# Linear attention feeding an MLP on one core: small per-head matmuls put into 64x64 quarters of the TensorE array

## The chip, the core and the metric

The kernel runs on one core of a Trainium2 chip. The metric is device time in microseconds for one execution. Before the change it is 293.32 us (median of three runs, 293.12 to 293.63). Line numbers such as L199 are lines of the kernel before the change, as the profile names them. PE is TensorE (PEld its weight loads), DVE is VectorE, ACT is ScalarE, POOL is GpSimd, SP is SyncE.

## What is computed

There are 8 batches of 8 heads, each with 576 tokens of 64 dimensions. Linear attention is followed by two dense layers with a tanh-shrink between them.

```python
phi = lambda x: np.where(x > 0, x, np.exp(x) - 1.0) + 1.0
q_p, k_p = phi(q), phi(k)
kv  = einsum('bhsd,bhse->bhde', k_p, v)          # 64x64 per head
z   = k_p.sum(axis=2)                            # 64 per head
num = einsum('bhsd,bhde->bhse', q_p, kv)
den = einsum('bhsd,bhd->bhs', q_p, z) + 1e-06
x   = (num / den) as 4608 tokens x 512 (head, dim)
h   = x @ w_in                                   # 512 -> 2048
out = (h - tanh(h)) @ w_out                      # 2048 -> 512
```

## The kernel before

**The dense part** runs over nine chunks `c` of 512 tokens. Layer 1 (`l1mm`, L366) makes 16 slices `fi` of 128 features, each from four 128x512 matmuls over the head pairs `p`; ACT takes the tanh of two slices at once (L372) and DVE subtracts (L373). Layer 2 (`l2mm`, L387) then makes four token blocks of 128 in 16 steps `s` of four matmuls each; ACT copies a finished block out (L396) and SP sends it (L401). One layer of one chunk is 64 matmuls.

**The attention part** runs over eight batches of 576 tokens and is slipped into the dense stream by hand. The lists `s1[fi]` and `s2[s]` say which pieces are issued after which slice of layer 1 or step of layer 2. Every engine works through its own instructions in program order, so the place in these lists is the place in each engine's queue. Chunk 0 carries batch 1; chunk `c` from 1 to 6 carries batch `c+1`; batch 0 comes before everything.

On the chip a batch lies as two partition halves (`hg`), two groups `i`, and two heads `h` beside each other, so its eight heads are (hg, i, h). The pieces that the change touches are these:

- **kv** (`a_kv_cols`, L199; for batch 1 `a_kv`, L177; for batch 0 `b0_kv`, L221, and `b0_z`, L210). For each group and each of nine token strips, two matmuls stand side by side in the array, one per partition half: 64 rows of contraction, 128 columns of weights (both heads of the strip), and both heads' `v` as the moving side. The result holds four 64x64 blocks of which two mix different heads. DVE multiplies it with a 0/1 `mask` (L202, L186, L225, L214) into `kz`, which takes the mixed blocks out. Each `v` carries columns of ones, so that z comes out as further columns. There are 36 such matmuls per batch.
- **den** (`a_den`, L276): sixteen matmuls of 32 weight columns, four side by side; DVE adds 1e-6 (L281) and takes the reciprocal (L285). `a_spread` sends it through DRAM and back to all partitions (`rdb`, L305 and L308); batch 1 splits it (`a_split`, L295 to L298) and spreads it with matmuls (L354).
- **num** (`num_mm`, L317 and L320; batch 0 L231): for each head pair `p` one 128x128x512 matmul whose weights are the masked `kz`, and four 64-column matmuls for the last 64 tokens. `a_num` issues pair after pair, one per layer-2 step (`s` 9 to 13, in chunk 1 `s` 12 to 15), in PSUM banks 6 and 7 in turn; DVE scales each into `xT` (L328, L333). For batch 1, ACT copies the five results (L344, L346).

**PSUM** has eight banks, `ps_all[:, 0..7]`. Dense work takes banks 0 to 5 in rotation, attention takes 6 and 7. In chunk 0 the side work takes 4 to 7 in rotation.

**Loads** are issued by POOL. `load_wi` (L110) loads `w_in` with two transfers per column slice, one for each 64 partitions, because a pair `p` holds head rows that lie 256 apart.

## Time and profile before

| | |
|---|---|
| median of three runs | 293.32 us |
| profiled execution: first to last instruction (its span) | 291.64 us |
| granted TensorE clock, mean | 0.999 |
| PE busy | 284.7 us (98%) |
| DVE, ACT, POOL busy | 175.1, 139.8, 34.0 us |
| dense matmuls L366 and L387 | 127.5 and 127.3 us busy |
| kv, batches 2 to 7 (L199) | 216 matmuls, 7.4 us busy |
| num (L317) | 28 matmuls, 10.1 us busy |
| num, last 64 tokens (L320) | 32 matmuls, 2.2 us busy |

Only the span of the profiled execution is on the page, and no time of its own around it; the median stands 1.68 us above the span. Busy times of PE count pipelined matmuls, which overlap, so a group's share of the path is read from where its first matmul and the next group's first matmul start, not from its mean duration. A wait is put down to the engine or transfer that ended last before it.

### The profile page before, as it was taken

Reading aid. Unit: us, or ns where it says so; the run is one execution under the profiler, and the core shown is the slowest. Engines: PE = TensorE matmul, PEld = TensorE weight load, DVE = VectorE, ACT = ScalarE, POOL = GpSimd, SP = SyncE. Lnnn points to the kernel's source line nnn. Section 1 sums busy time; section 2 is a strip of 40 time slices with the busy share of each in tenths; the row PEclk is TensorE's granted clock in tenths of the full one; section 3 lists DMA queues with packets and bytes.
Section 4 is the critical chain, followed back from the end, with each engine's and each line's share of the span. In section 5 each row is a group of like instructions: output and inputs, shape, how many; then the busy total and the mean of one; then the engine's idle time right before and its main releaser. Section 6 shows DMA issues by size and latency. Waiting matters only on the chain.

```text
span 291.6 us, 4505 instructions
## 1 busy us (share of the span) xinstructions
PE 284.7 (98%) x1803; PEld 134.4 (46%) x1803; DVE 175.1 (60%) x266; ACT 139.8 (48%) x168; POOL 34.0 (12%) x56
## 2 busy tenths in 40 slices
PE   7899999999999999999999999999999999999994
PEld 2544464454454444444454444444544444444443
DVE  4759968987468674776478637865581457106600
ACT  4838557846354734465345534751551155126411
POOL 8575030110030003000300030000000000000000
PEclk9999999999999999999999999999999999999999
DMA  6999999997998768965895579666117310130032
GB/s 98 192 203 213 207 205 211 212 180 141 257 165 152 176 127 136 197 145 123 136 223 125 122 138 197 136 150 139 31 38 165 73 36 0 42 84 20 0 74 72
DMA packets 39093, 38.94 MB, mean 134 GB/s; under 512 B 16352, under 2 KB 33824, under 8 KB 38304
## 3 DMA queue, kind: packets, MB, share of 16 engines
q0 software_dynamic: 17568, 18.35, 39.0%
q1 hardware_dynamic: 21344, 20.17, 30.7%
q8 instruction: 14, 0.23, 0.3%
q10 hardware_dynamic: 160, 0.13, 0.1%
q14 instruction: 7, 0.06, 0.1%
HBM read 43.91 MB, written 9.55 MB: 183 GB/s over the span
## 4 chain that ended last, share of the span: by engine, by line
PE 82%; DMA 13%; POOL 2%; ACT 1%; issue 1%; SPq 0%; DVE 0%; POOLq 0%
PE ps_all L366 38%; PE ps_all L387 37%; DMA v<-in_v_dram 6%; DMA w_in_sb<-in_moe_w_in_dram 3%; DMA kraw<-in_k_dram 2%; DMA out_dram<-osb 2%; PE ps_all L199 2%; PE ps_all L317 2%; PE ps_all L276 1%; POOL v L419 1%; ACT osb L396 1%; PE ps_all L177 1%; SPq L401 0%; POOL qraw L90 0%; PE ps_all L320 0%
## 5 line engine op out<-in xcount | busy, mean ns | idle before, releaser
L366 PE MATMUL ps_all<-xT,w_in_sb 128*128 128x512 bf16 x574 | 127.5, 379 | 0.0
L387 PE MATMUL ps_all<-w_out_sb,gT 128*128 128x512 bf16 x560 | 127.3, 379 | 0.0
L373 DVE TENSOR_TENSOR gT<-ps_all,th 128x1024 bf16<-128x1024 f32 x64 | 77.9, 1218 | 59.5 <-ACT th L372 59.5
L372 ACT ACTIVATE th<-ps_all 128x1024 f32<-128x1024 f32 x64 | 65.6, 1025 | 57.3 <-PE ps_all L366 47.2
L366 PEld LDWEIGHTS <-w_in_sb 128*128 128x128 bf16 x574 | 55.0, 98 | 66.0
L387 PEld LDWEIGHTS <-gT 128*128 128x128 bf16 x560 | 54.2, 98 | 64.5
L396 ACT COPY osb<-ps_all 128x512 f32<-128x512 f32 (+1 forms) x36 | 20.9, 583 | 71.8 <-PE ps_all L387 52.6
L328 DVE TENSOR_TENSOR xT<-ps_all,rdb 128x512 bf16<-128x512 f32 x24 | 16.5, 691 | 13.7 <-PE ps_all L317 11.2
L134 ACT ACTIVATE e<-qraw 128x1152 bf16<-128x1152 bf16 x16 | 18.5, 1161 | 8.5 <-DMA qraw<-in_q_dram 8.5
L134 ACT ACTIVATE e<-kraw 128x1152 bf16<-128x1152 bf16 x15 | 17.4, 1163 | 0.5 <-DMA kraw<-in_k_dram 0.5
L136 DVE TENSOR_TENSOR qp<-e,r 128x1152 bf16<-128x1152 bf16 x16 | 12.1, 759 | 8.0 <-ACT e L134 7.2
L136 DVE TENSOR_TENSOR kp<-e,r 128x1152 bf16<-128x1152 bf16 x15 | 11.4, 758 | 7.9 <-ACT e L134 7.0
L383 POOL COPY g<-qT 1x1 bf16<-1x1 bf16 x5 | 0.9, 178 | 118.9 <-DMA qT<-qp 118.9
L378 DVE TENSOR_TENSOR gT<-ps_all,th 128x512 bf16<-128x512 f32 x16 | 10.3, 686 | 2.4 <-ACT th L377 1.7
L377 ACT ACTIVATE th<-ps_all 128x512 f32<-128x512 f32 x16 | 9.2, 599 | 4.4 <-PE ps_all L366 3.2
L317 PE MATMUL ps_all<-qT,kz 128*128 128x512 bf16 x28 | 10.1, 379 | 0.0
L447 PE MATMUL ps_all<-zero 128*128 128x512 bf16 x29 | 8.2, 441 | 1.2 <-DVE zero L405 1.2
L135 DVE TENSOR_SCALAR r<-qraw 128x1152 bf16<-128x1152 bf16 x16 | 7.3, 454 | 2.1 <-DMA qraw<-in_q_dram 2.1
L199 PEld LDWEIGHTS <-kp 64*128 64x128 bf16 x216 | 6.4, 94 | 2.5 <-issue 2.5
L285 DVE RECIPROCAL rden<-den 128x144 f32<-128x144 f32 x7 | 7.4, 1053 | 0.2
L199 PE MATMUL ps_all<-vp,kp 64*128 64x136 bf16 x216 | 7.4, 220 | 0.0
L394 DVE COPY osb<-ps_all 128x128 f32<-128x128 f32 x1 | 0.3, 292 | 11.6 <-DMA out_dram<-osb 11.6
(85 smaller groups left out, 123.5 us busy)
## 6 DMA issues: line engine op xcount, KB each, us to landing
out_dram<-osb SPq DMA_DIRECT2D x70, 128.0 KB
rdb<-ds SPq DMA_DIRECT2D x12, 576.0 KB
kraw<-in_k_dram POOLq DMA_DIRECT2D x7, 576.0 KB, 6.7
qraw<-in_q_dram POOLq DMA_DIRECT2D x7, 576.0 KB, 8.8
v<-in_v_dram POOLq DMA_DIRECT2D x7, 576.0 KB, 11.8
w_in_sb<-in_moe_w_in_dram POOLq DMA_DIRECT2D x6, 256.0 KB, 8.8
w_out_sb<-in_moe_w_out_dram POOLq DMA_DIRECT2D x3, 512.0 KB, 14.3
qraw<-in_q_dram POOLq DMA_DIRECT2D x2, 288.0 KB, 4.6
```

Source lines behind the costliest of these rows:

```text
L134: return (lambda: nc.scalar.activation(e, x, AF.Exp), lambda: nc.vector.tensor_scalar(r, x, 0.0, 1.0, ALU.max, ALU.add), lambda: nc.vector ...
L136: lambda: nc.vector.tensor_tensor(y, e, r, ALU.min))
L199: nc.tensor.matmul(ps[hg][:, i, :], kp[r, i, j].rearrange("p h d -> p (h d)"), vp[r, i, j, :], start=(j == 0), stop=(j == J - 1))
L317: nc.tensor.matmul(ps, kz[:, p // 2, p % 2, 0:128], qT[:, p % 2, 0:8, p // 2, :], start=True, stop=True)
L328: nc.vector.tensor_mul(xT[:, p, S * b:S * b + 512].rearrange("p (j t c) -> p j t c", j=8, t=4), ps.rearrange("p j (t c) -> p j t c", t=4), ...
L366: nc.tensor.matmul(h, w_in_sb[:, 2 * (p % 2) + p // 2, fi * 128:(fi + 1) * 128], xT[:, p, c * 512:(c + 1) * 512], start=(n == 0), stop=(n ...
L372: nc.scalar.activation(th, h, AF.Tanh)
L373: nc.vector.tensor_sub(gT[:, fi:fi + 2, :], h, th)
L377: nc.scalar.activation(th, h, AF.Tanh)
L378: nc.vector.tensor_sub(gT[:, fi, :], h, th)
L387: nc.tensor.matmul(o, gT[:, fi, i * 128:(i + 1) * 128], w_out_sb[:, fi, :], start=(fi == 0), stop=(fi == NF - 1))
L396: nc.scalar.copy(osb[:, f0:f1], o[:, f0:f1])
```

## The change

The kv, z and num matmuls now work on one head each. A matmul has 64 rows and 64 columns of the array, and four of them, one per quarter, are issued after each other: two partition halves by two heads for kv and z, two heads by two partition halves for num. What used to be 36 matmuls of kv per batch are 72; what used to be 4 + 4 of num are 8 + 8. No block mixes heads any more, so `kz` is a plain copy and only the 32 columns for den are still multiplied with the (smaller) mask, now as two DVE operations for both halves together. `vp` holds 66 columns per head, the last two of ones.

`a_num` issues all matmuls of a batch in one place: the 8 large ones into banks 0 to 3, the 8 small ones into banks 6 and 7, and then all five DVE operations (after step `s` 9, in chunk 1 after `s` 12). Layer 2 takes banks 4 and 5 in turn, layer 1 takes bank `fi % 6`. In chunk 0 the order of the pieces after step 8 is den, the last tokens of batch 0, then num of batch 1, with the banks given below. A pair `p` now holds heads 2p and 2p+1, so `w_in` is loaded in its own row order with one transfer per slice, and the mask is filled for the new order. One of the two memsets of ones beside `v` (POOL, L419) is dropped, since only batch 1 still reads them.

```diff
     def load_wi(f0, n):
-        for h in range(2):
-            nc.gpsimd.dma_start(out=w_in_sb[64 * h:64 * h + 64, :, f0:f0 + n],
-                                in_=moe_w_in[256 * h:256 * h + 256, f0:f0 + n].rearrange(
-                                    "(t d) f -> d t f", d=64))
+        nc.gpsimd.dma_start(out=w_in_sb[:, :, f0:f0 + n],
+                            in_=moe_w_in[:, f0:f0 + n].rearrange("(t p) f -> p t f", p=128))
...
+    def quads():
+        return [(slice(64 * r, 64 * r + 64), slice(64 * c, 64 * c + 64), r, c) for c in range(2) for r in range(2)]
+
+    def kv_mm(b, v_of, ps_of):
         kp = kp_t[b]
         for i in range(2):
             for j in range(J):
-                for hg in range(2):
-                    r = slice(64 * hg, 64 * hg + 64)
-                    nc.tensor.matmul(ps[hg][:, i, :], kp[r, i, j].rearrange("p h d -> p (h d)"),
-                                     vp[r, i, j, :], start=(j == 0), stop=(j == J - 1))
-        for hg in range(2):
-            nc.vector.tensor_mul(kz_t[b][:, hg, :, 0:136], ps[hg], mask[:, hg, :, 0:136])
+                for rs, cs, hg, h in quads():
+                    nc.tensor.matmul(ps_of(cs, hg, i), kp[rs, i, j, h, :], v_of(rs, h, i, j),
+                                     start=(j == 0), stop=(j == J - 1))
...
+    def a_kv_cols(b, b0):
+        kz_t[b] = kz_c[b % 2]
+        kv_mm(b, lambda rs, h, i, j: vp[rs, i, j, h, :],
+              lambda cs, hg, i: ps_all[cs, b0 + hg, 66 * i:66 * i + 66])
+        ps = ps_all[:, b0:b0 + 2, 0:132].rearrange("p g (i e) -> p g i e", i=2)
+        nc.vector.tensor_mul(kz_t[b][:, :, :, 64:96], ps[:, :, :, 64:65].to_broadcast([128, 2, 2, 32]), mask)
+        nc.vector.tensor_copy(kz_t[b][:, :, :, 0:64], ps[:, :, :, 0:64])
...
+    def num_mm(b, i, bank_of):
+        kz, qT = kz_t[b], qT_t[b]
+        for rs, cs, h, hg in quads():
+            nc.tensor.matmul(ps_all[cs, bank_of(h), :].rearrange("p (j t) -> p j t", j=8), kz[rs, hg, i, 0:64],
+                             qT[rs, i, 0:8, hg, :], start=True, stop=True)
+
+    def rest_mm(b, b0, o):
+        kz, qT = kz_t[b], qT_t[b]
+        for i in range(2):
+            for rs, cs, h, hg in quads():
+                nc.tensor.matmul(ps_all[cs, b0 + h, 256 * i + o:256 * i + o + 64], kz[rs, hg, i, 0:64],
+                                 qT[rs, i, 8, hg, :], start=True, stop=True)
...
+    def a_num(b):
         rdb = rdb_t[b]
+        for i in range(2):
+            num_mm(b, i, lambda h: 2 * h + i)
+        rest = rest_mm(b, 6, 0)
+        for n in range(NP):
             nc.vector.tensor_mul(
+                xT[:, n, S * b:S * b + 512].rearrange("p (j t c) -> p j t c", j=8, t=4),
+                ps_all[:, n, :].rearrange("p (j t c) -> p j t c", j=8, t=4),
+                rdb[:, n, :, 0:8, :].rearrange("p t j c -> p j t c"))
...
             def num1():
-                sub["ns"] = new_ns(1)
-                for p in (NP, 0, 1, 2, 3):
-                    a_num_copy(1, sub["ns"], p, side)
+                ns = sub["ns"] = new_ns(1)
+                nc.scalar.copy(ns[:, :, 8, :], rest_mm(1, 6, 64))
+                for i in range(2):
+                    b0 = 4 + 2 * i
+                    num_mm(1, i, lambda h: b0 + h)
+                    nc.scalar.copy(ns[:, i::2, 0:8, :].rearrange("p a j t -> p a (j t)"), ps_all[:, b0:b0 + 2, :])
...
-            s2[7].append(lambda: (a_qT_pe(1, 0, side), a_kv(1, side), a_qT_pe(1, 1, side)))
-            s2[8].append(lambda: (b0_scale_rest(side), a_den(1, side), num1(), a_split(1)))
+            s2[7].append(lambda: (a_qT_pe(1, 0, Banks([4, 5])), a_kv(1, 6), a_qT_pe(1, 1, Banks([4, 5]))))
+            s2[8].append(lambda: (a_den(1, 4), scale_rest(0, 6, rdb_t[0]), num1(), a_split(1)))
...
-            s1[8 if c == 1 else 5].append(lambda: a_kv_cols(n1, attn))
-            s1[10 if c == 1 else 8].append(lambda: (a_den(n1, attn), a_spread(n1)))
-            for p in range(NP + 1):
-                s2[min(12 + p, 15) if c == 1 else 9 + p].append(lambda p=p: a_num(n1, p))
+            s1[8 if c == 1 else 5].append(lambda: a_kv_cols(n1, 6))
+            s1[10 if c == 1 else 8].append(lambda: (a_den(n1, 6), a_spread(n1)))
+            s2[12 if c == 1 else 9].append(lambda: a_num(n1))
```

Batch 1's `a_kv` uses the same `kv_mm` with the head's 64 columns of `v` and 64 columns of ones, so its matmuls have 128 moving columns where they had 192. Batch 0's `b0_kv`, `b0_z` and `b0_num` are rewritten in the same way.

More of the change, by code (lines that the diff above doesn't have):

```diff
@@ L60, in __call__ @@
             return ps_all[:, self.order[(self.n - 1) % len(self.order)], :]
-    dense = Banks([0, 1, 2, 3, 4, 5])
-    attn = Banks([6, 7])
     ident = const.tile([128, 128], BF16, name="ident")
-    mask = const.tile([128, 2, 2, 160], F32, name="mask")
+    mask = const.tile([128, 2, 2, 32], F32, name="mask")
     sel = const.tile([128, NP, 2, 64], F32, name="sel")
@@ L76 @@
     w_out_sb = const.tile([128, NF, DM], BF16, name="w_out_sb")
-    kz_c = [const.tile([128, 2, 2, 160], BF16, name=f"kz{i}") for i in range(2)]
+    kz_c = [const.tile([128, 2, 2, 96], BF16, name=f"kz{i}") for i in range(2)]
     v_b = [const.tile([128, 3, 2, J, D], BF16, name=f"v{i}") for i in range(2)]
-    vp = const.tile([128, 2, J, 136], BF16, name="vp")
+    vp = const.tile([128, 2, J, 2, 66], BF16, name="vp")
     k_t, q_t = {}, {}
@@ L170, in a_qT_pe @@
                 nc.vector.tensor_copy(dst, src)
-    def kv_mm(b, i, ps):
-        kp, vt = kp_t[b], v_b[b % 2]
-        for j in range(J):
-            for hg in range(2):
-                r = slice(64 * hg, 64 * hg + 64)
-                nc.tensor.matmul(ps[hg], kp[r, i, j].rearrange("p h d -> p (h d)"),
-                                 vt[r, :, i, j, :], start=(j == 0), stop=(j == J - 1))
-    def a_kv(b, banks):
-        kz_t[b] = kz_c[b % 2]
-        ps = [banks()[:, 0:384].rearrange("p (i e) -> p i e", i=2) for hg in range(2)]
-        for i in range(2):
-            kv_mm(b, i, [ps[hg][:, i, :] for hg in range(2)])
-        for hg in range(2):
-            nc.vector.tensor_mul(kz_t[b][:, hg], ps[hg][:, :, 0:160], mask[:, hg])
@@ L188, in a_vp @@
-    def a_vp(b, i):
-        nc.vector.tensor_copy(vp[:, i, :, 0:128].rearrange("p j (h d) -> p h j d", h=2), v_b[b % 2][:, 0:2, i])
-    def a_kv_cols(b, banks):
+    def quads():
+        return [(slice(64 * r, 64 * r + 64), slice(64 * c, 64 * c + 64), r, c) for c in range(2) for r in range(2)]
+    def kv_mm(b, v_of, ps_of):
         kp = kp_t[b]
-        kz_t[b] = kz_c[b % 2]
-        ps = [banks()[:, 0:272].rearrange("p (i e) -> p i e", i=2) for hg in range(2)]
         for i in range(2):
@@ L196, in a_kv_cols @@
             for j in range(J):
-                for hg in range(2):
-                    r = slice(64 * hg, 64 * hg + 64)
-                    nc.tensor.matmul(ps[hg][:, i, :], kp[r, i, j].rearrange("p h d -> p (h d)"),
-                                     vp[r, i, j, :], start=(j == 0), stop=(j == J - 1))
-        for hg in range(2):
-            nc.vector.tensor_mul(kz_t[b][:, hg, :, 0:136], ps[hg], mask[:, hg, :, 0:136])
+                for rs, cs, hg, h in quads():
+                    nc.tensor.matmul(ps_of(cs, hg, i), kp[rs, i, j, h, :], v_of(rs, h, i, j),
+                                     start=(j == 0), stop=(j == J - 1))
@@ new lines, in a_kv, with a_vp @@
+    def a_kv(b, b0):
+        kz_t[b], vt = kz_c[b % 2], v_b[b % 2]
+        kv_mm(b, lambda rs, h, i, j: vt[rs, h:3:2 - h, i, j, :],
+              lambda cs, hg, i: ps_all[cs, b0 + hg, 128 * i:128 * i + 128].rearrange("p (a e) -> p a e", a=2))
+        ps = ps_all[:, b0:b0 + 2, 0:256].rearrange("p g (i e) -> p g i e", i=2)
+        nc.vector.tensor_mul(kz_t[b][:, :, :, 64:96], ps[:, :, :, 64:96], mask)
+        nc.vector.tensor_copy(kz_t[b][:, :, :, 0:64], ps[:, :, :, 0:64])
+    def a_vp(b, i):
+        nc.vector.tensor_copy(vp[:, i, :, :, 0:64].rearrange("p j h d -> p h j d"), v_b[b % 2][:, 0:2, i])
@@ L205, in b0_z @@
+    def a_kv_cols(b, b0):
[4 more added lines that the diff above has]
+        nc.vector.tensor_mul(kz_t[b][:, :, :, 64:96], ps[:, :, :, 64:65].to_broadcast([128, 2, 2, 32]), mask)
+        nc.vector.tensor_copy(kz_t[b][:, :, :, 0:64], ps[:, :, :, 0:64])
     def b0_z(i):
         for j in range(J):
-            for hg in range(2):
-                r = slice(64 * hg, 64 * hg + 64)
-                nc.tensor.matmul(ps_all[:, 4 - 2 * i + hg, 0:32], kp_t[0][r, i, j].rearrange("p h d -> p (h d)"),
-                                 one[r, 0:32], start=(j == 0), stop=(j == J - 1))
+            for rs, cs, hg, h in quads():
+                nc.tensor.matmul(ps_all[cs, 4 - 2 * i + hg, 0:32], kp_t[0][rs, i, j, h, :],
+                                 one[rs, 0:32], start=(j == 0), stop=(j == J - 1))
@@ L213, in b0_zc @@
     def b0_zc(i):
-        nc.vector.tensor_mul(kz_t[0][:, :, i, 128:160], ps_all[:, 4 - 2 * i:6 - 2 * i, 0:32], mask[:, :, i, 128:160])
+        nc.vector.tensor_mul(kz_t[0][:, :, i, 64:96], ps_all[:, 4 - 2 * i:6 - 2 * i, 0:32], mask[:, :, i, :])
     def b0_kv(i):
         for j in range(J):
-            for hg in range(2):
-                r = slice(64 * hg, 64 * hg + 64)
-                nc.tensor.matmul(ps_all[:, 2 * i + hg, 0:128], kp_t[0][r, i, j].rearrange("p h d -> p (h d)"),
-                                 v_b[0][r, 0:2, i, j, :], start=(j == 0), stop=(j == J - 1))
+            for rs, cs, hg, h in quads():
+                nc.tensor.matmul(ps_all[cs, 2 * i + hg, 0:64], kp_t[0][rs, i, j, h, :],
+                                 v_b[0][rs, h, i, j, :], start=(j == 0), stop=(j == J - 1))
@@ L224, in b0_kz @@
     def b0_kz(i):
-        nc.vector.tensor_mul(kz_t[0][:, :, i, 0:128], ps_all[:, 2 * i:2 * i + 2, 0:128], mask[:, :, i, 0:128])
+        nc.vector.tensor_copy(kz_t[0][:, :, i, 0:64], ps_all[:, 2 * i:2 * i + 2, 0:64])
+    def num_mm(b, i, bank_of):
[3 more added lines that the diff above has]
+                             qT[rs, i, 0:8, hg, :], start=True, stop=True)
@@ L227, in b0_num @@
+    def rest_mm(b, b0, o):
[4 more added lines that the diff above has]
+                                 qT[rs, i, 8, hg, :], start=True, stop=True)
+        return ps_all[:, b0:b0 + 2, :].rearrange("p h (i x) -> p (h i) x", i=2)[:, :, o:o + 64]
     def b0_num(i, ns):
-        kz, qT, b0 = kz_t[0], qT_t[0], 2 * i
-        for hg in range(2):
-            nc.tensor.matmul(ps_all[:, b0 + hg, :].rearrange("p (j t) -> p j t", j=8), kz[:, hg, i, 0:128],
-                             qT[:, i, 0:8, hg, :], start=True, stop=True)
+        b0 = 2 * i
+        num_mm(0, i, lambda h: b0 + h)
@@ L259, in b0_rest, with scale_rest, a_den @@
         rdb_t[0] = rdb
-    def b0_scale_rest(banks):
-        ps = num_mm(0, NP, banks)
+    def scale_rest(b, b0, rdb):
         nc.vector.tensor_mul(
-            xT[:, :, 512:576].rearrange("p a (t c) -> p a t c", t=4),
-            ps[:, 0:NP, :].rearrange("p a (t c) -> p a t c", t=4), rdb_t[0])
-    def a_den(b, banks, parts=range(4)):
+            xT[:, :, S * b + 512:S * b + 576].rearrange("p a (t c) -> p a t c", t=4),
+            rest_mm(b, b0, 0).rearrange("p a (t c) -> p a t c", t=4), rdb)
+    def a_den(b, bank, parts=range(4)):
         kz, qT = kz_t[b], qT_t[b]
-        ps = banks()[:, 0:J * 16]
+        ps = ps_all[:, bank, 0:J * 16]
         for t in range(4) if b == 0 else ():
@@ L275, in a_den @@
                 for t in range(4):
-                    nc.tensor.matmul(ps[32 * t:32 * t + 32], kz[:, p // 2, p % 2, 128:160],
+                    nc.tensor.matmul(ps[32 * t:32 * t + 32], kz[:, p // 2, p % 2, 64:96],
                                      qT[:, p % 2, :, p // 2, 16 * t:16 * t + 16],
@@ L311, in a_spread @@
         rdb_t[b] = rdb
-    def num_mm(b, p, banks):
-        kz, qT = kz_t[b], qT_t[b]
-        ps = banks().rearrange("p (j t) -> p j t", j=8)
-        if p < NP:
-            nc.tensor.matmul(ps, kz[:, p // 2, p % 2, 0:128], qT[:, p % 2, 0:8, p // 2, :], start=True, stop=True)
-        else:
-            for a in range(NP):
-                nc.tensor.matmul(ps[:, a, :], kz[:, a // 2, a % 2, 0:128], qT[:, a % 2, 8, a // 2, :],
-                                 start=True, stop=True)
-        return ps
-    def a_num(b, p):
+    def a_num(b):
         rdb = rdb_t[b]
-        ps = num_mm(b, p, attn)
-        if p < NP:
+        for i in range(2):
+            num_mm(b, i, lambda h: 2 * h + i)
+        rest = rest_mm(b, 6, 0)
+        for n in range(NP):
             nc.vector.tensor_mul(
-                xT[:, p, S * b:S * b + 512].rearrange("p (j t c) -> p j t c", j=8, t=4),
-                ps.rearrange("p j (t c) -> p j t c", t=4),
-                rdb[:, p, :, 0:8, :].rearrange("p t j c -> p j t c"))
-        else:
-            nc.vector.tensor_mul(
-                xT[:, :, S * b + 512:S * b + 576].rearrange("p a (t c) -> p a t c", t=4),
-                ps[:, 0:NP, :].rearrange("p a (t c) -> p a t c", t=4), rdb[:, :, :, 8, :])
+                xT[:, n, S * b:S * b + 512].rearrange("p (j t c) -> p j t c", j=8, t=4),
+                ps_all[:, n, :].rearrange("p (j t c) -> p j t c", j=8, t=4),
+                rdb[:, n, :, 0:8, :].rearrange("p t j c -> p j t c"))
+        nc.vector.tensor_mul(
+            xT[:, :, S * b + 512:S * b + 576].rearrange("p a (t c) -> p a t c", t=4),
+            rest.rearrange("p a (t c) -> p a t c", t=4), rdb[:, :, :, 8, :])
     def new_ns(b):
         return rpool.tile([128, NP, J, 64], F32, name="ns", tag="rdb")
-    def a_num_copy(b, ns, p, banks):
-        ps = num_mm(b, p, banks)
-        if p < NP:
-            nc.scalar.copy(ns[:, p, 0:8, :], ps)
-        else:
-            nc.scalar.copy(ns[:, :, 8, :], ps[:, 0:NP, :])
     def a_spread_pe(b, bank0, pairs):
@@ L365, in l1mm @@
     def l1mm(c, fi, h, p, n):
-        nc.tensor.matmul(h, w_in_sb[:, 2 * (p % 2) + p // 2, fi * 128:(fi + 1) * 128], xT[:, p, c * 512:(c + 1) * 512],
+        nc.tensor.matmul(h, w_in_sb[:, p, fi * 128:(fi + 1) * 128], xT[:, p, c * 512:(c + 1) * 512],
                          start=(n == 0), stop=(n == NP - 1))
@@ L417 @@
     load_q(1)
-    for i in (1, 0):
-        nc.gpsimd.memset(v_b[i][:, 2], 1.0)
-    nc.gpsimd.memset(vp[:, :, :, 128:136], 1.0)
+    nc.gpsimd.memset(v_b[1][:, 2], 1.0)
+    nc.gpsimd.memset(vp[:, :, :, :, 64:66], 1.0)
     load_v(1)
@@ L428 @@
     nc.vector.memset(mask, 0.0)
-    for hh in range(2):
-        nc.vector.memset(mask[64 * hh:64 * hh + 64, :, :, 64 * hh:64 * hh + 64], 1.0)
-        for p in range(NP):
-            m = 128 + 4 * hh + p
-            nc.vector.memset(mask[64 * hh:64 * hh + 64, p // 2, p % 2, m:m + 1], 1.0)
+    for h in range(2):
+        for hg in range(2):
+            for i in range(2):
+                m = 4 * hg + 2 * h + i
+                nc.vector.memset(mask[64 * h:64 * h + 64, hg, i, m:m + 1], 1.0)
     for n in (1, 2):
-        nc.vector.tensor_copy(mask[:, :, :, 128 + 8 * n:136 + 8 * n], mask[:, :, :, 128:136])
+        nc.vector.tensor_copy(mask[:, :, :, 8 * n:8 * n + 8], mask[:, :, :, 0:8])
     nc.vector.memset(one, 1.0)
@@ L474 @@
     b0_kz(0)
-    a_den(0, Banks([4]))
+    a_den(0, 4)
     ns0 = new_ns(0)
@@ L512 @@
         if c == 0:
-            side = Banks([4, 5, 6, 7])
             sub = {}
@@ L521, in num1 @@
             def num1():
-                sub["ns"] = new_ns(1)
-                for p in (NP, 0, 1, 2, 3):
-                    a_num_copy(1, sub["ns"], p, side)
+                ns = sub["ns"] = new_ns(1)
+                nc.scalar.copy(ns[:, :, 8, :], rest_mm(1, 6, 64))
+                for i in range(2):
+                    b0 = 4 + 2 * i
+                    num_mm(1, i, lambda h: b0 + h)
+                    nc.scalar.copy(ns[:, i::2, 0:8, :].rearrange("p a j t -> p a (j t)"), ps_all[:, b0:b0 + 2, :])
             s1[11].append(lambda: a_kphi(1, 0))
@@ L578 @@
                     for p, fi in part_:
-                        nc.tensor.matmul(hs[fi][:, 256 * x:256 * x + 256], w_in_sb[:, 0, fi * 128:(fi + 1) * 128],
+                        nc.tensor.matmul(hs[fi][:, 256 * x:256 * x + 256], w_in_sb[:, p, fi * 128:(fi + 1) * 128],
                                          xT[:, p, 256 * x:256 * x + 256], start=(x == 0), stop=False)
@@ L587 @@
         for fi in range(4 if c == 0 else 0, NF):
-            h = first() if c == 0 else dense()
+            h = first() if c == 0 else ps_all[:, fi % 6, :]
             if c == 2 and fi == 1:
                 for two in (0, 2):
-                    for f, o in ((0, ps_all[:, dense.order[(dense.n - 2) % 6], :]), (1, h)):
+                    for f, o in ((0, ps_all[:, 0, :]), (1, h)):
                         for p in (two, two + 1):
@@ L600 @@
             elif fi % 2:
-                n = dense.order[(dense.n - 1) % 6]
+                n = fi % 6
                 l1act2(fi - 1, ps_all[:, n - 1:n + 1, :], gT)
@@ L609 @@
             if g == 0:
-                os_[i] = ps_all[:, i, :] if c == 0 else dense()
+                os_[i] = ps_all[:, i if c == 0 else 4 + i % 2, :]
             if c == NC - 1 and i == 3:
                 if g == 0:
-                    o2 = dense()
+                    o2 = ps_all[:, 0, :]
                     for o, f in ((os_[i], slice(0, 384)), (o2, slice(384, DM))):
```

## The prediction

> **What bounds the kernel now.** I read the page's parts 1, 2 and 4 first.

> ```profile
> PE 284.7 (98%) x1803; PEld 134.4 (46%) x1803; DVE 175.1 (60%) x266; ACT 139.8 (48%) x168; POOL 34.0 (12%) x56
> PEclk9999999999999999999999999999999999999999
> ...
> PE 82%; DMA 13%; POOL 2%; ACT 1%; issue 1%; SPq 0%; DVE 0%; POOLq 0%
> ```

> PE is busy 98% of the span at full clock, and the chain that ended last is PE. Written out in time, that chain is PE matmuls without a break from 38.9 to 277.5 us, and PE also ran without a break from 17.9 us. So from 17.9 us on a nanosecond of PE time is a nanosecond of the result, unless a new wait is made. The question is what the attention matmuls cost PE as inserts into the dense stream. I read that from the starts in the timeline of PE around one kv and one den (columns: start, length, engine, line, count):

> ```profile
> 57.83 0.38 PE L366 MATMUL ps_all<-xT,w_in_sb 128*128 128x512 bf16 x1
> 58.14 1.24 PE L199 MATMUL ps_all<-vp,kp 64*128 64x136 bf16 x36
> 59.31 1.90 PE L366 MATMUL ps_all<-xT,w_in_sb 128*128 128x512 bf16 x8
> 61.14 0.43 PE L276 MATMUL ps_all<-qT,kz 128*32 128x144 bf16 x16
> 61.51 0.82 PE L366 MATMUL ps_all<-xT,w_in_sb 128*128 128x512 bf16 x3
> ```

> The pace of a stream comes from the chain of waits: 64 matmuls L387 in 13.81 us are 216 ns each for 512 columns, four L320 in 0.12 us are 29 ns each for 64 columns (80.51 to 80.63 in the timeline). So a matmul takes 0.417 ns per moving column plus 2 ns. Now kv: the last L366 starts at 57.83, the next kind at 58.14, 0.31 later instead of 0.216: about **0.1 us to leave the full array**. The insert ends at 59.31, so it cost 59.31 - 57.83 - 0.216 = 1.26 us. Two L199 stand side by side and take 136 columns, 59 ns; 18 pairs are 1.06, and the remaining 0.20 is the two changes of shape. Den agrees: 61.51 - 61.14 = 0.37 for four groups of four; 4 x 62 ns (144 columns) are 0.25, and 0.1 is the way back. L276 thus shows four column strips side by side at full pace, L199 two row halves. Num is in the full array: four L317 at 0.216 and four L320 at 0.029 are 0.98 us per batch, with no change of shape.

> **Part 1, kv of batches 2 to 7.** Removed: 18 pairs, 1.06 us. Added: 18 quads, each of time Q. The two changes of shape stay. A quarter matmul has 66 columns, 30 ns if all four run side by side; that is Q's lower end. The upper end is the new weight loads. Loads of 128 columns in pairs keep up with 25 ns:

> ```profile
> 12.65 0.40 PE L210 MATMUL ps_all<-one,kp 64*128 64x32 bf16 x18
> 12.98 0.25 PE L272 MATMUL ps_all<-one,eps 128*32 128x144 bf16 x4
> ```

> From 12.65 to 12.98 is 0.33, less 0.1 for the change, over 9 pairs: 25 ns per pair, 12.5 per matmul. Four matmuls with four loads of their own, if two pairs' loads had to follow each other, would be 50; if none overlapped, 100. L276 loads four 32-column strips within its 62 ns. I take Q = 36 ns, near the streaming row, because L276 has exactly this pattern (four loads, four streams) and shows no time for loads beyond streaming. Gain per batch: 1.06 - 18 x 0.036 = 0.41 us (0.52 at Q = 30; 0.16 at 50; a loss of 0.74 at 100).

> **Part 2, num of batches 2 to 7.** Removed 0.98 us. Added: four quarters of 512 columns twice, 2 x 0.216 = 0.43; two quads of 64 columns, 2Q = 0.07; and a new insert that leaves the full array and returns, 0.20, paid once because all stands in one place. Sum 0.70, gain 0.28 (0.25 at Q = 50, 0.15 at 100).

> Six batches: 6 x (0.41 + 0.28) = **-4.1 us** (-4.8 at 30, -2.5 at 50).

> **Part 3, chunk 0 (batch 1).** kv there goes from 192 columns (82 ns x 18 = 1.48) to 128 (56 ns x 18 = 1.00): -0.48. But the order behind it changes, and here I see a new wait:

> ```profile
> 42.08 0.43 PE L276 MATMUL ps_all<-qT,kz 128*32 128x144 bf16 x16
> 42.58 1.03 PE L317 MATMUL ps_all<-qT,kz 128*128 128x512 bf16 x4
> 43.44 1.89 PE L387 MATMUL ps_all<-w_out_sb,gT 128*128 128x512 bf16 x8
> 45.37 0.30 PE L354 MATMUL ps_all<-w,sel 32*128 32x144 bf16 x8
> ```

> ```profile
> 42.19 0.42 DVE L263 TENSOR_TENSOR xT<-ps_all,rdb 128x256 bf16<-128x256 f32 x1 [0.37 <-PE ps_all L320]
> 42.57 0.31 DVE L281 TENSOR_SCALAR den<-ps_all 128x144 f32<-128x144 f32 x1
> 42.91 1.05 DVE L285 RECIPROCAL rden<-den 128x144 f32<-128x144 f32 x1
> 44.00 0.23 DVE L295 CAST t<-rden 128x144 bf16<-128x144 f32 x1
> ```

> Today batch 0's last tokens are scaled (L263) before den. After the change den comes first, so DVE does add, 1.05 us of reciprocal, and only then that scaling, which reads banks 6 and 7. The second half of num writes whole banks 6 and 7 and must wait for it; the first half writes bank 4 and waits for the add. Counting from den's first matmul (0): den streams 0.25 and is readable at about 0.45; add until 0.80; reciprocal until 1.9; scaling until 2.3. PE: den, a change of shape (0.1), 16 small quarters (0.15) by 0.5; first half of num from 0.85 to 1.07; second half not before 2.4, then 0.216 and 0.1 back: dense work resumes at 2.7. Before, the block ran from 41.87 (L320) to 43.44, 1.57 us; after, 0.1 + 2.7 = 2.8: +1.26. The spread L354 had 0.11 us of wait for `w` (45.37 against 43.44 + 7 x 0.216 + 0.31 = 45.26), which is now hidden: -0.11. Behind the waiting matmul stand layer 2's steps 9 to 15, which nothing else delays. Chunk 0 in all: -0.48 + 1.26 - 0.11 = **+0.66 us** (-0.92 without the wait: the block would then be 0.1 + 0.25 + 0.1 + 0.15 + 0.43 + 0.1 = 1.13 where it was 1.57).

> **Part 4, what costs nothing.** Batch 0: z keeps its 25 ns or doubles to 50, `b0_kv` falls from 56 to 36 per group of four; over nine groups each, -0.2 to +0.2 us. It is covered by v(1): L177 waited for that transfer (38.86), and DMA is 97 to 99% busy in the slices up to there, so arriving earlier gains at most the 0.15 us waited. POOL issues five `w_in` transfers instead of ten (0.65 us each, 3 us less) and one memset of 1.08 us less; the same bytes pass a DMA side that is full, so I take 0, between -0.3 and +0.3. DVE: per batch 2 x 0.43 (L202) becomes about 0.3 + 0.42; hidden, DVE is at 60%. `a_num`'s five operations in a row occupy 4 x 0.69 + 0.42 = 3.2 us after step 9; the head of the next layer 1 is six steps away (5.2 us). In chunk 1 it is three steps, 2.6 us: there the first starts at 77.8 after `rdb`'s landing, the fourth ends at 80.6, and layer 1 needs it at about 81.4. Covered by 0.8 us; each us that `rdb` lands later beyond that costs one, once. Layer 2 in two banks: a block's evacuation of 0.59 us has 3.45 us. ACT saves 0.4 us in chunk 0, hidden.

> **Sum.** -4.1 + 0.66 + 0 = -3.5 us. The profiled execution's span is 291.64, so 288.1; the 1.68 us between it and the median lie outside the span and stay. **Forecast 289.8 us.**

> **The rivals.** *A, loads of a quad in two steps* (Q = 50). Gain 2.5 - 0.66: 291.5 us. For it: no row of 64-column loads exists. Against: L276's four loads. [...]

> *B, slower: the quads are limited per matmul.* If loads or issue put matmuls one after another, each of the 72 counts. The point from which it decides: 6 x (1.06 + 0.98 - 0.63 - 20Q) = 0.66, Q = 65 ns or 16 ns per matmul. Shown rates lie at 12.5 (L210) and 15.6 ns (L276), for 18 and 16 matmuls, which is close, and no burst of 72 exists. At Q = 100: 6 x (0.74 - 0.15) = +3.5; chunk 0's 0.66, and 0.8 more for its kv (1.80 where 1.00 was counted); batch 0 about +0.9 (18 quads, 0.04 to 0.075 more each, less the 0.15 us of wait): 299.2 us. [...]

> *C, the quarters don't run side by side*: num goes to 8 x 0.216 + 8 x 0.029 + 0.20 = 2.2 us, kv to 72 x 0.030 = 2.2, in chunk 0 to 72 x 0.056 = 4.0: 6 x (1.2 + 1.1) + 3 = +17, 310 us. L199 and L276 speak against it, each for one direction.

> *D, the wait in chunk 0 doesn't arise*: 0.66 + 0.92 = 1.6 us better, 288.2.

> *E, a new wait in chunk 1* (`rdb` lands 3 us later): +2.2, 292.0.

> **How the numbers follow.** Forecast 0.50, A 0.18, B 0.17, C 0.03, D 0.06, E 0.06. B and C are slower by over 0.2% (0.6 us, about what a measurement of this kernel can tell from no change); between A and B, Q near 60 gives no change. Faster 0.72, same 0.06, slower 0.22. The range takes in Q = 30 with D (293.3 - 4.8 - 0.9 = 287.6), A and E, and reaches partly into B: 287.6 to 294.8.

> **What would show it.** In the new profile: kv inserts with 0.85 us between dense matmuls instead of 1.26 (over 1.26: B); one num insert of 0.70; PE idle of about 0.35 and 1.3 us around 42 us, released by DVE L281's and L263's successors; no other PE idle after 18 us. The forecast is wrong if Q is above 50, or if PE shows idle at the head of a layer 1.

## The result, and the profile after

The changed kernel takes **295.37 us** (median of four runs, 294.45 to 295.63) where the kernel before took 293.33 (four runs beside them, 293.12 to 293.63): a ratio of 1.0063, 95% interval 1.0046 to 1.0079. It is slower by 2.0 us where 3.5 less was forecast, a little above the range's upper end of 294.8. The profiled execution of it is the 294.45 one, with a span of 292.7; before it was 291.64. The other three differ from it in the granted clock (0.988 against 0.993), which is taken up under the clock, below.

The page's parts 1, 2 and 4 of the changed kernel:

```profile
PE 281.2 (96%) x2191; PEld 130.9 (45%) x2191; DVE 170.5 (58%) x264; ACT 139.4 (48%) x166; POOL 30.2 (10%) x50
PEclk9989999999999999999999999999999999999999
...
PE 89%; DMA 5%; issue 2%; POOL 1%; DVE 1%; ACT 1%; SPq 0%; DVEq 0%; POOLq 0%
```

PE is busy for 3.5 us less and the span is 1.0 longer, so PE now idles. One slice of the clock shows less than full speed, and there are 388 more matmuls. What PE waited for, from its table of waits (in total, times, longest):

```profile
PE ps_all L248 <- issue: 2.9, 1, 2.9
PE ps_all L233 <- DVE xT L270: 1.7, 1, 1.7
```

The second wait is the one forecast for chunk 0. The first was in no step of the prediction: "issue" means that nothing which the profile records held PE back. In the timeline of PE it stands inside one loop, between the eighth and the ninth of sixteen matmuls that are all alike and wait for nothing (columns: start, length, engine, line, count, idle before):

```profile
13.90 0.48 PE L215 MATMUL ps_all<-v,kp 64*64 64x64 bf16 x36
14.99 0.50 PE L248 MATMUL ps_all<-rden,sel 32*128 32x128 f32 x8 [0.61 <-DVE kz L219]
18.39 0.50 PE L248 MATMUL ps_all<-rden,sel 32*128 32x128 f32 x8 [2.90 <-issue]
...
21.62 1.70 PE L357 MATMUL ps_all<-xT,w_in_sb 128*128 128x512 bf16 x5
```

Up to 14.99 us the new kernel is level with the old one (its spread, L240, began at 14.93). The dense stream begins at 21.62 where it began at 17.85.

**Where the time went**, from the starts of the same work in both timelines (late is positive):

| step | change |
|---|---|
| start of the dense stream, 17.85 to 21.62 | +3.77 |
| half clock behind the gap, less 0.16 of wait for `v` that is now hidden | +0.28 |
| chunk 0: kv -0.46; block with den, num +1.88; spread -0.09 | +1.33 |
| batches 2 to 7, kv and num | -4.33 |
| sum (the two spans differ by 1.04) | +1.05 |

The gap of 2.90 us is the larger part of the +3.77. Most of the rest arises from 18.39 to 21.62 us, where the granted clock was 0.50 from 19.15 on.

### The profile page after: what moved, and what is told of

The parts are those of the page before. It is cut to its first block, busy times and chain, and to the rows that moved or that the text cites. A ratio compares the mean times of both kernels' runs of the same rounds, so it can differ in the third digit from the quotient of the medians.

```text
span 292.7 us, 5280 instructions
## 1 busy us (share of the span) xinstructions
PE 281.2 (96%) x2191; PEld 130.9 (45%) x2191; DVE 170.5 (58%) x264; ACT 139.4 (48%) x166; POOL 30.2 (10%) x50
## 4 chain that ended last, share of the span: by engine, by line
PE 89%; DMA 5%; issue 2%; POOL 1%; DVE 1%; ACT 1%; SPq 0%; DVEq 0%; POOLq 0%
PE ps_all L357 43%; PE ps_all L378 39%; DMA v<-in_v_dram 3%; DMA out_dram<-osb 2%; PE ps_all L177 2%; PE ps_all L225 1%; PE ps_all L283 1%; PE ps_all L248 1%; ACT osb L387 1%; POOL kraw L87 0%; SPq L392 0%; POOL qraw L87 0%; DVE rden L292 0%; PE ps_all L159 0%; PE ps_all L570 0%
## 5 line engine op out<-in xcount | busy, mean ns | idle before, releaser
L357 PE MATMUL ps_all<-xT,w_in_sb 128*128 128x512 bf16 x574 | 127.9, 380 | 0.0
L378 PE MATMUL ps_all<-w_out_sb,gT 128*128 128x512 bf16 x560 | 124.1, 379 | 0.0
L357 PEld LDWEIGHTS <-w_in_sb 128*128 128x128 bf16 x574 | 55.2, 98 | 66.2 <-issue 0.8
L387 ACT COPY osb<-ps_all 128x512 f32<-128x512 f32 (+1 forms) x36 | 20.9, 584 | 72.1 <-PE ps_all L378 47.1
L327 DVE TENSOR_TENSOR xT<-ps_all,rdb 128x512 bf16<-128x512 f32 x24 | 14.9, 683 | 9.2 <-PE ps_all L225 6.7
L437 PE MATMUL ps_all<-zero 128*128 128x512 bf16 x29 | 8.9, 467 | 1.2 <-DVE zero L396 1.2
L90 POOL DMA_DIRECT2D qraw<-in_q_dram x7 | 5.4, 773 | 17.4 <-DVE r L130 16.7
L385 DVE COPY osb<-ps_all 128x128 f32<-128x128 f32 x1 | 0.3, 292 | 11.6 <-DMA out_dram<-osb 11.6
L130 DVE TENSOR_SCALAR r<-kraw 128x1152 bf16<-128x1152 bf16 x15 | 6.8, 452 | 0.0
L177 PEld LDWEIGHTS <-kp 64*64 64x64 bf16 x504 | 5.0, 106 | 2.6 <-issue 2.1
## 6 DMA issues: line engine op xcount, KB each, us to landing
w_in_sb<-in_moe_w_in_dram POOLq DMA_DIRECT2D x3, 512.0 KB, 13.4
```

The lines of the kernel that those rows point to most:

```text
L130: lambda: nc.vector.tensor_scalar(r, x, 0.0, 1.0, ALU.max, ALU.add),
L177: nc.tensor.matmul(ps_of(cs, hg, i), kp[rs, i, j, h, :], v_of(rs, h, i, j), start=(j == 0), stop=(j == J - 1))
L327: nc.vector.tensor_mul(xT[:, n, S * b:S * b + 512].rearrange("p (j t c) -> p j t c", j=8, t=4), ps_all[:, n, :].rearrange("p (j t c) -> p ...
L357: nc.tensor.matmul(h, w_in_sb[:, p, fi * 128:(fi + 1) * 128], xT[:, p, c * 512:(c + 1) * 512], start=(n == 0), stop=(n == NP - 1))
L378: nc.tensor.matmul(o, gT[:, fi, i * 128:(i + 1) * 128], w_out_sb[:, fi, :], start=(fi == 0), stop=(fi == NF - 1))
L387: nc.scalar.copy(osb[:, f0:f1], o[:, f0:f1])
```

## The experiments

The theory, **S** (supply): PE reads its program in blocks that a DMA brings, and the change puts so many short matmuls at the start that PE reaches the end of a block before the next one is there. In the trace an instruction transfer on queue q8 (16 KB) ran from 15.97 to 16.94 us, into PE's gap; in the kernel before one ran from 16.42 to 17.37 and PE waited there only 0.22 us, for DVE. Rivals: **F**, the fp32 matmuls L248 stall behind 64x64 ones; **W**, the new `w_in` transfers (one for two) load the DMA differently; and a **limit of rate**, PE or its sequencer not keeping up with that many instructions.

### Batch 0 back in pairs

```diff
-            for rs, cs, hg, h in quads():
-                nc.tensor.matmul(ps_all[cs, 4 - 2 * i + hg, 0:32], kp_t[0][rs, i, j, h, :],
-                                 one[rs, 0:32], start=(j == 0), stop=(j == J - 1))
+            for hg in range(2):
+                r = slice(64 * hg, 64 * hg + 64)
+                nc.tensor.matmul(ps_all[:, 4 - 2 * i + hg, 0:32], kp_t[0][r, i, j].rearrange("p h d -> p (h d)"),
+                                 one[r, 0:32], start=(j == 0), stop=(j == J - 1))
...
```

The same is done to `b0_kv`, with two copies that take each head's block out of the mixed result.

> The changed kernel with batch 0's z and kv matmuls put back as pairs with 128 weight columns (18 instead of 36 matmuls each time, 144 PE instructions fewer before the first dense matmul); its two diagonal blocks are copied by two DVE operations. Theory S (PE runs out of instructions): the 2.9 us in which PE waits for nothing visible at 15.5 us vanishes, and so does the half-clock stretch behind it; the dense stream starts at about 18.0 us instead of 21.6, time 290.5 to 291.5 us. Rival F (the fp32 spread stalls behind 64x64 matmuls or because of what DVE and ACT do there): num of batch 0 is still in quarters and w_in is still loaded in one transfer, so if the cause is there the gap stays and the time stays at 294.5 to 295.6 us.

Measured: 291.66 us (290.29 to 291.74), ratio 0.9924 (0.9901 to 0.9947). The gap is gone and the dense stream begins at 17.95. All the rest of the change stays, so the loss at the start comes from batch 0's z and kv alone. The wait of 1.67 us in chunk 0 stays as well. The median lies 0.16 us above the expectation and the profiled run 0.2 below it; the clock, below, bears on this.

### The old `w_in` transfers

```diff
-        nc.gpsimd.dma_start(out=w_in_sb[:, :, f0:f0 + n],
-                            in_=moe_w_in[:, f0:f0 + n].rearrange("(t p) f -> p t f", p=128))
+        for h in range(2):
+            hs = slice(64 * h, 64 * h + 64)
+            nc.gpsimd.dma_start(out=w_in_sb[hs, :, f0:f0 + n],
+                                in_=moe_w_in[:, f0:f0 + n].rearrange("(t p) f -> p t f", p=128)[hs])
```

> The changed kernel with w_in loaded again by two transfers per slice, 64 partitions each, same rows and bytes. Theory S: the gap of 2.5 to 3.5 us at 15 us stays, since as many PE instructions are used up and the transfers are the same bytes; 294.5 to 295.7 us. Rival W (the larger and earlier w_in transfers of the change are what delays PE): the gap shrinks by more than half, time about 292 us.

Measured: 295.52 us (295.01 to 295.69), ratio 1.0062 (1.0045 to 1.0079), with a gap of 2.83 us at the same place. W falls.

### Sixteen small matmuls more, ahead of everything

```diff
+    for _ in range(16):
+        nc.tensor.matmul(ps_all[:, 0, 0:16], zero[:, 0:128], zero[:, 0:16], start=True, stop=True)
```

> The changed kernel with 16 matmuls of 16 columns of zeros (32 PE instructions) added behind the first 18 warming matmuls, where PE waits for q anyway. Theory S: the place of the gap is fixed by the count of instructions, so it moves 32 instructions earlier in the program, from the middle of the first fp32 spread into the second b0_kv, with 8 of its 36 matmuls left; PE resumes at about 18.4 us as before, time 295 to 297 us. Rival F: the gap stays in the fp32 spread, behind its first eight records.

Measured: 295.01 us (one run). The gap moved back to other work, into the second `b0_kv`:

```profile
13.63 0.39 PE L215 MATMUL ps_all<-v,kp 64*64 64x64 bf16 x28
17.72 0.32 PE L215 MATMUL ps_all<-v,kp 64*64 64x64 bf16 x8 [3.70 <-issue]
```

Between the two places lie 8 matmuls of `b0_kv` and 8 of L248: sixteen. F falls, since PE now stops among plain bf16 quarters; the place follows the number of instructions.

### The old kernel with only batch 0 in quarters

```diff
-                nc.tensor.matmul(ps_all[:, 4 - 2 * i + hg, 0:32], kp_t[0][r, i, j].rearrange("p h d -> p (h d)"),
-                                 one[r, 0:32], start=(j == 0), stop=(j == J - 1))
+                for h in range(2):
+                    cs = slice(64 * h, 64 * h + 64)
+                    nc.tensor.matmul(ps_all[cs, 4 - 2 * i + hg, 0:32], kp_t[0][r, i, j, h, :],
+                                     one[r, 0:32], start=(j == 0), stop=(j == J - 1))
...
```

`b0_kv` likewise; each quarter still takes both heads' `v`, as the pairs did.

> The kernel before with one part of the change alone: batch 0's z and kv matmuls with 64 weight columns each (36 instead of 18, 144 PE instructions more before the first dense matmul), everything else as before. Theory S: the gap appears in the old kernel too, 3 us long, in the first fp32 spread, behind about ten of its sixteen records (four instructions later than in the changed kernel, since num of batch 0 has four fewer instructions); dense work starts near 21.6 us; 296.5 to 298.0 us. Rival: if the gap needs another part of the change (one w_in transfer, num in quarters, DVE's copies), it doesn't appear and the time is 293 to 293.7.

Measured: 297.72 us (296.91 to 297.85), ratio 1.0141 (1.0126 to 1.0156). A gap of 2.77 us stands in the first spread, and the dense stream begins at 21.48. This one part, put into the old kernel, costs 4.3 us.

### More instructions, but earlier

```diff
-    spin(18)
+    spin(9)
+    for _ in range(80):
+        nc.tensor.matmul(ps_all[:, 0, 0:64], zero[:, 0:128], zero[:, 0:64], start=True, stop=True)
```

> The changed kernel with 142 PE instructions MORE, all of them early: 9 of the first 18 warming matmuls are replaced by 80 matmuls of 64 columns of zeros, over about the same time. Theory S with blocks of 256 instructions that are asked for when the block before is entered: the second block is now entered at about 1 us, so the third is asked for while the transfers are still few, and the boundary that starved PE at 15.2 us is now passed at about 12.8 us with its block long there; the fourth is needed only at about 27 us. The gap vanishes although there are more instructions: dense work at about 18.0 us, time 290.3 to 291.8, like e1_b0_pairs. Rival (PE is simply given too many instructions, a rate limit): the gap stays or grows, 295.4 us or more.

Measured: 292.29 us (291.11 to 293.1), ratio 0.9959 (0.9939 to 0.998). With 71 matmuls more than the changed kernel the gap is gone, and the limit of rate falls with it. The instruction transfer ran from 10.87 to 11.84 us. The median lies above the expectation, which only the profiled run (291.11) met, and PE has a wait that was not expected:

```profile
13.11 0.48 PE L215 MATMUL ps_all<-v,kp 64*64 64x64 bf16 x36 [1.59 <-DMA v<-in_v_dram]
```

In the changed kernel this stands at 12.21, so `v` landed 0.9 us later. The block's transfer of 0.97 us now runs while `v` is loaded. That it pushes `v` back is argued from that, and not tested.

### The loads behind the first slice held back

```diff
-    for f0, n in ((0, 256), (256, 256), (512, 512), (1024, 512), (1536, 512)):
-        load_wi(f0, n)
-    load_k(1)
...
+    load_wi(0, 256)
...
+    gz = rpool.tile([1, 1], BF16, name="gz")
+    nc.gpsimd.tensor_copy(gz, kz_t[0][0:1, 0, 1, 64:65])
+    for f0, n in ((256, 256), (512, 512), (1024, 512), (1536, 512)):
+        load_wi(f0, n)
+    load_k(1)
...
```

POOL issues the loads only when it has read a number of batch 0's second z, at about 13 us.

> The changed kernel with all POOL loads behind the first w_in slice held back until batch 0's second z is ready (a POOL copy of one element waits for it at about 13.4 us), so that few transfers are queued from 12 to 14 us. If the instruction block is late because its transfer stands among the loads, it is moved before 15 us instead of from 15.97 to 16.94, and the gap of 2.9 us in the first fp32 spread shrinks below 1 us or goes. If its time is fixed, or fixed by how far PE has got, the gap stays at 2.5 us or more. The whole time isn't the question here: the held-back loads come later, and dense work may wait for them.

Measured: 293.64 us (one run). From 13 to 15 us the DMA share is 0.73 where it was 1.45, the instruction transfer starts at 13.76 instead of 15.97, and the gap shrinks from 2.90 to 0.83:

```profile
14.63 0.50 PE L248 MATMUL ps_all<-rden,sel 32*128 32x128 f32 x8 [0.60 <-DVE kz L219]
15.96 0.81 PE L248 MATMUL ps_all<-rden,sel 32*128 32x128 f32 x8 [0.83 <-issue]
```

With the same instructions and fewer loads queued, the block comes 2.2 us earlier and PE goes on 2.4 us earlier. In finer stretches the DMA is still full behind the boundary here too (share 1.43 from 13.25 to 13.50 us), and the transfer starts as the loads run out (1.04 from 13.50 to 13.76, then 0.56 to 14.00). It takes 0.98 us beside a nearly idle DMA (0.15 from 14.00 to 14.75) where it took 0.97 among the loads. So what the loads hold up is its start, by this one run.

**What all of these have in common** is a count. The table by stretches counts PE's matmuls and weight loads from the start of the span up to the point where PE stopped. Each row has the stretch, its length, and then busy time and count (after x) of PE, of PEld and of the other engines. The rows are the changed kernel, then the sixteen added, the old kernel with batch 0 in quarters, and the loads held back.

```profile
0.00:18.35 18.35, 12.84 (x223) 6.50 (x223) 8.24 (x32) 10.10 (x16) 13.60 (x24) 1.00 1.03 157
```

```profile
0.00:17.65 17.65, 12.62 (x222) 6.60 (x224) 7.99 (x31) 10.08 (x16) 12.99 (x24) 0.97 1.02 157
```

```profile
0.00:18.20 18.20, 13.89 (x223) 7.09 (x223) 9.46 (x34) 10.26 (x16) 12.93 (x24) 1.00 1.03 157
```

```profile
0.00:15.90 15.90, 12.83 (x223) 6.53 (x223) 8.10 (x32) 10.08 (x16) 8.65 (x18) 1.00 0.93 141
```

446 recorded instructions in each, at four different times and in two different loops (`b0_kv` and the spread). How long a block is can be read at the end of the kernel before, from the starts of its last two instruction transfers, 249.74 and 277.39 us:

```profile
0.00:249.74 249.74, 246.59 (x1612) 116.31 (x1613) 164.99 (x257) 126.98 (x152) 33.95 (x56) 1.00 0.78 147
0.00:277.39 277.39, 274.24 (x1740) 128.88 (x1741) 174.79 (x265) 137.53 (x164) 33.95 (x56) 1.00 0.72 137
```

### Chunk 0 in the old order

```diff
-            s2[8].append(lambda: (a_den(1, 4), scale_rest(0, 6, rdb_t[0]), num1(), a_split(1)))
+            s2[8].append(lambda: (scale_rest(0, 6, rdb_t[0]), a_den(1, 4), num1(), a_split(1)))
```

> The changed kernel with the last tokens of batch 0 again ahead of den in chunk 0. Theory of the forecast for this stage: DVE's scaling no longer stands behind the reciprocal, the 1.67 us wait of the small num matmuls for DVE goes, and the block from its first matmul to the next dense one takes 1.5 to 2.0 us instead of 3.35; 1.3 to 1.9 us better than the changed kernel in the span behind 45 us, 293.3 to 294.2 us in all with the gap at 15 us untouched. Rival: the waits for ACT's copy and for den's add take its place, and the block stays above 2.7 us, time above 294.6.

Measured: 293.12 us (ten runs, 292.27 to 294.69), ratio 0.9996 (0.9979 to 1.0013). The gap at the start stays (3.0 us). In chunk 0 DVE scales batch 0's last tokens before den, and PE's wait falls from 1.67 to 0.17 us:

```profile
45.83 0.26 PE L233 MATMUL ps_all<-qT,kz 64*64 64x64 bf16 x8
46.02 0.43 PE L283 MATMUL ps_all<-qT,kz 128*32 128x144 bf16 x16
46.62 0.26 PE L233 MATMUL ps_all<-qT,kz 64*64 64x64 bf16 x8 [0.17 <-DVE xT L270]
...
47.69 1.68 PE L378 MATMUL ps_all<-w_out_sb,gT 128*128 128x512 bf16 x7
```

The block takes 1.86 us instead of 3.35, so 1.5 come from the order of den and the scaling. The median falls by 2.25, which is more than that and a little more than expected.

### Both, and the shortest repair

Batch 0 in pairs with the old order; then the early small matmuls with the old order; then only batch 0's z in pairs (72 instructions fewer, `b0_kv` stays in quarters) with the old order. Their edits are those above.

> Both repairs together: batch 0's z and kv in pairs as in e1_b0_pairs, and the last tokens of batch 0 ahead of den as in e4_rest_first. If the two losses are separate they add up: the dense stream starts at about 18 us, the block in chunk 0 takes about 1.9 us instead of 3.35, six batches keep their 0.72 us each. 290.3 (the undisturbed run of e1_b0_pairs) less 1.4 = 288.7 to 289.3 us. If three of four runs of e1_b0_pairs were at 291.7 because the 1.67 us wait in chunk 0 brought a stretch of half clock, that spread goes as well. Rival: the chunk-0 gain is used up by a wait behind it, 290 us or more.

Measured: 288.63 us (288.39 to 288.98), ratio 0.9838 (0.9823 to 0.9853). The two repairs add up, and a little more than was expected.

> e7_more_early with the order of e4_rest_first: all matmuls of the change stay in quarters, both losses removed. If theory S and the order account hold, 288.5 to 289.3 us, within 0.3 us of e5_pairs_and_order; above 293 us if e7_more_early keeps its gap.

Measured: 289.82 us (289.57 to 290.1), ratio 0.9875 (0.9858 to 0.9891). It misses its expectation by 0.5 us. PE's wait for `v` is 1.61 us here, where the changed kernel has 0.42; that this is the reason is argued and not tested.

> The changed kernel with only batch 0's z in pairs again (72 PE instructions fewer before the first dense matmul, kv of batch 0 stays in quarters) and the order of e4_rest_first. Theory S: the boundary moves 72 instructions later, to about the twelfth dense matmul, which PE reaches at about 20.5 us, after the block has come (18.4); no gap, half of the instructions are enough. 288.3 to 289.2 us, like e5_pairs_and_order. Rival (the gap grows with the number of small matmuls, without a boundary): half the gap stays, about 290.5.

Measured: **288.39 us** (288.31 to 288.5), ratio 0.983 (0.9814 to 0.9846) against 293.34: the fastest, and ahead of both kernels. The count in it is the finest test of S:

```profile
0.00:18.18 18.18, 15.72 (x223) 8.04 (x223) 10.48 (x37) 10.99 (x17) 13.59 (x24) 1.00 1.05 163
```

The same 446 are counted up to 18.18 us, but here PE has hardly stopped. The 446th belongs to the fourth dense matmul (the expectation had the twelfth), which starts at 17.73. The next one starts at 18.19, 0.46 us later, where a matmul of 512 columns takes 0.216. So about 0.24 us is left of the gap. It shows best in PE's weight loads:

```profile
18.18 1.41 PEld L358 LDWEIGHTS <-w_in_sb 128*128 128x128 bf16 x8 [0.57 <-issue]
```

PE goes on 1.25 us after the transfer's end (16.93), as it did behind the long gaps. With 72 instructions fewer, its own work from boundary to boundary takes 6.3 us (11.6 to 17.95), nearly as long as the block takes to come (6.5), so there is nothing to spare. A cost in proportion to the instructions would have left half of the 2.9 us.

**The clock.** These runs also say what a gap brings with it. In the profiled execution of the changed kernel the granted clock is 0.50 from 19.15 to 22.56 us. With the old order in chunk 0 that stretch is twice as long: the mean clock is 0.70 from 15.0 to 18.0 us and 0.64 from 18.0 to 24.9, which makes 6.8 us at half clock. With the old `w_in` transfers, the sixteen matmuls added and the loads held back the mean clock of the profiled execution is 0.988, as in that run (0.993 in the changed kernel), so the stretch is put at 6.8 us there too, by estimate. The wait in chunk 0 seems to do the same in most executions. Among the kernels that keep that wait and have no gap at the start (batch 0 in pairs; more, but earlier) seven of nine executions had a mean clock of 0.994 or 0.988; among those without it (the last three) one of twelve had 0.994, the others 0.997 or more. A stretch of 3.41 us (19.15 to 22.56) costs up to 1.7 us by estimate (half of it), which would explain why the order is worth 1.3 and 1.0 us between the profiled executions of these pairs, but 3.0 and 2.5 between their medians. Where in those executions the clock fell isn't seen, as only one of each was profiled.

## Why the prediction was wrong, step by step

**Parts 1 and 2, right.** Kv and num of one later batch:

```profile
62.13 1.46 PE L357 MATMUL ps_all<-xT,w_in_sb 128*128 128x512 bf16 x6
63.52 0.78 PE L177 MATMUL ps_all<-vp,kp 64*64 64x66 bf16 x72
64.23 1.90 PE L357 MATMUL ps_all<-xT,w_in_sb 128*128 128x512 bf16 x8
```

```profile
77.66 4.48 PE L378 MATMUL ps_all<-w_out_sb,gT 128*128 128x512 bf16 x20
82.07 0.63 PE L225 MATMUL ps_all<-qT,kz 64*64 64x512 bf16 x8
...
82.69 2.76 PE L378 MATMUL ps_all<-w_out_sb,gT 128*128 128x512 bf16 x12
```

The last L357 starts at 62.13 + 5 x 0.216 = 63.21, so the kv insert is 64.23 - 63.21 - 0.216 = 0.80 us (0.85 forecast, 1.26 before). Num is 82.69 - (77.66 + 19 x 0.216) - 0.216 = 0.71 (0.70 forecast, 0.98 before). Six batches gave 4.33 us, 4.1 forecast. From the first to the last start of L177 the quads follow each other every 33 ns, for 36 taken. That decides A, B and C: no second step of loads, no 16 ns per matmul, no quarters one after another. Loads of 64 columns can have cost 3 ns per quad at most, since streaming alone was put at 30. B's Q = 100 was an estimate, four loads of 25 ns one after another; four tiles side by side took 8 ns per matmul (L205).

**Part 3, right in mechanism, too small.** Forecast +0.66, measured +1.33. The wait came from L270 as said, but one matmul group earlier. PE and DVE of the changed kernel in chunk 0:

```profile
45.56 0.43 PE L283 MATMUL ps_all<-qT,kz 128*32 128x144 bf16 x16
45.92 0.26 PE L233 MATMUL ps_all<-qT,kz 64*64 64x64 bf16 x8
47.84 0.26 PE L233 MATMUL ps_all<-qT,kz 64*64 64x64 bf16 x8 [1.67 <-DVE xT L270]
...
48.57 0.41 PE L225 MATMUL ps_all<-qT,kz 64*64 64x512 bf16 x4 [0.25 <-ACT ns L512]
48.91 1.90 PE L378 MATMUL ps_all<-w_out_sb,gT 128*128 128x512 bf16 x8
```

```profile
46.12 0.31 DVE L288 TENSOR_SCALAR den<-ps_all 128x144 f32<-128x144 f32 x1 [0.89 <-PE ps_all L283]
46.46 1.05 DVE L292 RECIPROCAL rden<-den 128x144 f32<-128x144 f32 x1
47.43 0.36 DVE L270 TENSOR_TENSOR xT<-ps_all,rdb 128x256 bf16<-128x256 f32 x1
```

The step that failed is "16 small quarters (0.15) by 0.5": eight are batch 0's, but the other eight are batch 1's `rest_mm`, which write banks 6 and 7 while L270 still has other columns of them to read. They wait to 47.84, and the first half of num (forecast at 0.85 after den, in the shadow of the wait) stands behind them in PE's order. Then ACT must copy bank 6 and 7 (0.25) before the second half. So the block, from den's first matmul, is 3.35 us where 2.7 was forecast; with the 0.1 for the change of shape ahead of it that is 3.45 for 2.8, or +1.88 against the 1.57 before. (The prediction writes +1.26 for 2.8 less 1.57, which is 1.23.) The kv there fell by 0.46 (0.48 forecast), and the spread's wait by 0.09 (0.11).

**Part 4, the step that turned the sign.** "Batch 0 ... -0.2 to +0.2 us" counted the time of the matmuls, and that was right: the first spread began at 14.99 where it began at 14.93. The step put no price on the 144 added instructions (72 matmuls with a load each) as instructions. But a block of instructions that PE ran through in 14 us (12.8 to 27.0) now took it 3.1, and the transfer of the next block, which had already been 3.6 us late in starting, became what PE waited for: +3.77 with the half clock up to 21.62, and about 0.45 more from the half clock behind it. The wait for `v` that was to cover this stage took up only 0.16 of it. The row was there to be read in the profile before (part 3's q8, 14 packets, and where they ran), and the prediction never asked who waits for it. The rival that ended on the slow side, B, was about the rate of short matmuls, not about their supply; it also counts 18 quads for batch 0 where z and `b0_kv` together have 36. The 97 to 99% that the step gives for the DMA stand in no view: the page's digits say 90% or more. `w_in` in one transfer, POOL, DVE, `a_num`'s five operations and layer 2's two banks cost nothing that the trace shows: PE has no idle time at the head of a layer 1, so E did not arise.

**D** (288.2 us without the wait in chunk 0) is what the two repaired kernels came to, 288.4 and 288.6. The forecast of 289.8 is met by neither: with the start repaired and the order kept the kernel takes 291.66 (290.29 in the profiled run). That the kernel with the early matmuls and the old order measured 289.82 is chance: it has no wait in chunk 0 and a longer one for `v`.

Open: the trace doesn't show when a block is asked for, so that it is asked for at the boundary is argued from the times. Nor does it show what PE does between the end of the transfer and its next instruction (1.45 us here, 1.47 with sixteen added, 1.22 with the loads held back). Whether the wait of `rest_mm` is one for the bank or could be avoided with other columns was not tried.

## What to carry to other kernels

A change that cuts matmuls into smaller ones must be counted in instructions too: find the instruction queue's transfers in the trace, count matmuls and loads between them, and compare the time in which PE will run that many (256 here) with the time that a block takes to come (here 6 us while the loads fill the DMA, 4 where they ran out on the way). Where dense work gave that time the quarters paid (4.33 us over six batches); at the start, with full queues, fewer and larger instructions were better here, even though they compute twice as much (288.4 and 288.6 us against 289.8). An idle stretch of PE that the profile puts down to "issue", in the middle of a loop of like instructions, was the sign of it here (2.90 us).

## What the runs showed of the hardware that was not expected

- An instruction block waited for the loads: by the count of 256, its transfer started 3.6 to 4.3 us after the boundary with full queues (DMA share 1.3 to 1.4), about 3 us where the boundary was placed early (1.2), and 1.8 us after it where the loads ran out just then (one run).
- The price wasn't in proportion to the instructions: 72 fewer left 0.24 of the 2.9 us, and 142 more, placed earlier, left nothing. What counted was whether PE's work on one block lasted as long as the next one took to come (3.1 against 6.1 us in the changed kernel, 6.3 against 6.5 with 72 fewer).
- Four 64x64 tiles side by side took a quad of 66 columns every 33 ns, and of 32 columns (L205: 36 matmuls in 0.28 us from first to last start) 8 ns per matmul.
- Gaps of 2.8 to 3.7 us on PE went with 3.4 or 6.8 us of half clock; one of 0.83 us (with 0.60 ahead of it) with 6.8 as well, and a wait of 1.6 us for `v` somewhat earlier with none.
